# Value projection turned around: weights stationary, 512 positions moving, results turned in 32x32 blocks on the way to memory

## The chip, the core and the metric

The kernel runs on one core of a Trainium2 chip. The metric is the device time of one execution in microseconds (us). The engines of the core are named as the profile names them: PE (matrix products; PEld is its loading of the stationary operand), DVE (vector), ACT (activation), POOL (general), SP (issues transfers). Each has its own queue of instructions and works through it in order; engines wait for each other through semaphores. Transfers (DMA) are issued from the queues of SP, ACT or POOL and carried out by 16 DMA engines.

## What is computed

Two attentions of 32 heads of width 18 over the same 2048 positions of width 576, mixed by a gate:

```python
def _A_ref(x, wqkv, wo):                      # every head has its own q, k, v
    qkv = (x @ wqkv).reshape(B, S, 3, H, Dh)
    p = softmax(einsum("bhqd,bhkd->bhqk", q, k) * Dh ** -0.5)
    return einsum("bhqk,bhkd->bhqd", p, v)  ...  @ wo

def _B_ref(x, wq, wk, wv, wo):                # 32 query heads share one k and one v
    ...

g = sigmoid((x * gate_w).sum(-1, keepdims=True))
return g * a + (1 - g) * b
```

S = 2048, D = 576, H = 32, Dh = 18. All inputs and outputs are float32. The change concerns v of the first attention: 2048 positions by 576 features (32 heads of 18).

## The kernel before, in words

**Units.** The 64 heads are 64 units, u = 0 to 63: the 32 of the shared-key attention (they use the value tile vb), then the 32 with their own keys and values. One step T handles one tile of 128 key positions of one unit, so that there are 1024 steps; the main loop goes two steps at a time. A unit's scores are computed twice: once with queries as stationary operand, only to find each query's maximum (step_max, L525 to L555; the matmul is L540), and, 22 steps later (LEAD), with keys stationary, followed by the exponential on ACT (exps, L586) and the product with the values (step_pv, L614). A block of values of the second attention is the stationary operand of L614: 19 columns, 18 features and a column of ones that sums the probabilities.

**Matrix products in float32.** A product of two float32 tensors is made of three: each operand is split into a high and a low part, and high by high, high by low and low by high are added up. With a contraction over 576 this makes the list PROJ (L37) of 14 matmuls for one result tile. products (L264) runs that list with 128x128 weights stationary and 512 positions of x moving. This is how keys and queries are projected, in 14 weight tiles (MT) by 4 position blocks (project, L339; project_rest, L427).

**The value projection** (project_v, L316) takes it the other way round: 128 positions of x are stationary, and half of the value weights, 288 columns, move. A result tile has positions on the partitions and 288 features along them. There are 32 such units (16 position tiles, 2 halves), each of 14 matmuls (L319). ACT copies a result from PSUM into a tile with 19 columns per head (L322), whose 19th column a memset has filled with ones at the start (L314), and issues on its own queue the transfer to the DRAM tensor v_d (L323), which holds 16 x 128 x (32 x 19) values. The value weights come in as two tiles of 288 columns during the key and query projection (L447 to L454) and are split by ACT and DVE.

**When.** The value units run in the lead, the iterations T = -22 to T = -2, in which only maxima are computed. The text LEADS gives the order of an iteration: "mA0 MA1 mA2 MA3 V.A mB0 MB1 mB2 MB3 V.B". Each m is one maximum matmul (512 keys), followed by a reduction on DVE (L555). V stands for as many value units as keep to the schedule:

```python
while len(vunits) > 32 * (-T - 1 - (c == "B")) // LEAD:
```

So there are 22 half-steps, and each gets one or two units. The maxima of a half-step use PSUM banks 4, 5, 6 and one of the banks 0 to 3; value units take banks 0 to 3 in turn (next_s, next_m). From T = 0 on a written-out order for each pair of steps (FIRST, PLAIN, ONE, TWO, EACH) interleaves scores (s), maxima (m), one maximum over two key blocks at once (c, with its helper x) and value products (p), each with its bank.

**At T = 0** (open_ph2, L494) the pools of the projection are closed and those of the main loop opened in their room; the first two key tiles then get two rows of a constant each (L505). The values of four heads at a time are loaded by load_vg (L509), one transfer of 608 KB, 30 steps before their first use.

**Maxima to score rows.** At the end of a unit's maxima, max_rows (L557) reduces and turns them on DVE, splits them on POOL (L565 to L567), and writes them through a DRAM tensor m_d into two extra rows of the query tile (L569 to L573), all on SP's queue. The scores of that unit, six steps later, need them. Queries of units 3 and up are loaded on SP's queue too (load_q, L124 and L855). A list "slow" advances one piece per iteration, among them the gates (L464).

Of the kernel before, what the change touches and what calls it, by code (L numbers as in the profile page):

```python
# [8 lines left out]
F32 = mybir.dt.float32  # L9
# [40 lines left out]
def gated_mix_kernel(ctx: ExitStack, tc: tile.TileContext, xT, wall, wv, wo, out):  # L50
# [21 lines left out]
    v_d = dram.tile([16, P, H * 19], F32, name="v_d")  # L72
    on_d = [dram.tile([9 * P, S], F32, name=f"on{x}") for x in "hl"]


# [28 lines left out]
    def other():  # L104
        return bk[:, next_s(), :]
# [84 lines left out]
    def load_w(mt, eng=None):  # L190
        st = wpool.tile([P, NKT, P], F32, name="wst", bufs=MT - 2)
        load5(st, wall[mt], eng)
        return st

    def size(n, st):
        for k0, k1, p in ((0, 4, P), (4, 5, 64)):
            nc.vector.tensor_reduce(n[0:p, k0 // 4:k0 // 4 + 1], st[0:p, k0:k1], axis=AX.XY, op=OP.max,
                                    apply_absolute_value=True)
# [110 lines left out]
        nc.vector.tensor_copy(vb[:, 4 * c:4 * c + 4, 0:18],  # L309
                              pv[:, 0:72].rearrange("p (j d) -> p j d", d=18))  # L310

    vst = [vsp.tile([P, 16, 19], F32, name=f"vst{i}") for i in range(3)]
    for t in vst:
        nc.gpsimd.memset(t, 1.0)  # L314

    def project_v(st_, hf, w):  # L316
        fp = other()
        for n, (a, b, k, kr) in enumerate(PROJ):
            nc.tensor.matmul(fp[:, 0:288], X[b][:kr, k, st_ * P:(st_ + 1) * P], w[a][:kr, k, :],  # L319
                             start=(n == 0), stop=(n == len(PROJ) - 1))  # L320
        t = vst[st_ % 3]
        nc.scalar.activation(t[:, :, 0:18], fp[:, 0:288].rearrange("p (h d) -> p h d", d=18), AF.Copy)  # L322
        dma(v_d[st_, :, 304 * hf:304 * hf + 304], t.rearrange("p h d -> p (h d)"), nc.scalar)  # L323

    def run(gen):
        for _ in gen:
# [23 lines left out]
    with tc.tile_pool(name="xs", bufs=6, side="right") as xsp:  # L350
# [61 lines left out]
        for n in range(6, 12):  # L412
# [8 lines left out]
    vwp = ph1.enter_context(tc.tile_pool(name="vwp", bufs=1, side="right"))  # L421
    VS = [None, None]

    for b in (SB, MB):
        dma(ksb[b + 54:b + 56, :], ones_r, nc.gpsimd)

    def project_rest():  # L427
        bal = None
        for n in range(12, len(JOBS)):
            mt, c = JOBS[n]  # L430
            if c == 0 and mt + 1 < MT:
                WP.append(prep_w(W[mt + 1]))
            project(n, gen=bal, at={16: (2, 11)}.get(n, ()))
            for m in range(*AT.get(n, (0, 0))):
                measure_a(m, W[m])
            if n == 13:
                bal = balance(2)
                next(bal)
            if c == 0:
                if mt == 4:  # L440
                    load_k(ksb, ROW_KB, nc.gpsimd)
                    load_kd(kdb, ROW_KB, nc.gpsimd)
                if mt == 5:
                    load_q(0, nc.gpsimd)
                if mt in (6, 7):
                    load_q(mt - 5, nc.gpsimd)
# [47 lines left out]
    def open_ph2():  # L494
        ph1.close()
        L["pt"] = ctx.enter_context(tc.tile_pool(name="ppool", bufs=1, side="left")).tile([P, 16, 512], F32, name="pt")
        L["work"] = ctx.enter_context(tc.tile_pool(name="work", bufs=2, side="left"))
        p2 = ctx.enter_context(tc.tile_pool(name="p2", bufs=1, side="right"))
        L["pool"] = p2
        L["ks"] = [p2.tile([P, S], F16, name=f"ksa{i}") for i in range(2)] + [ksb]  # L500
        L["kds"] = [p2.tile([P, 512], F16, name="kda"), kdb]
        L["oacc"] = p2.tile([P, 16, D], F32, name="oacc")
        for t in L["ks"][:2]:
            for b in (SB, MB):
                dma(t[b + 54:b + 56, :], ones_r)  # L505

    VG = {}
# [49 lines left out]
    def max_rows(u):  # L557


        m = ms[u % 2]  # L560
        nc.vector.tensor_reduce(m[:, 0:16], MX.pop(u), axis=AX.X, op=OP.max, negate=True)
        mt = lead.tile([P, 32], F32, name="mt")
        nc.vector.transpose(mt, m)  # L563
# [3 lines left out]
        nc.gpsimd.tensor_tensor(mh[:, 1, :], mt, mh[:, 0, :], op=OP.subtract)  # L567
        md = m_d[u % 4]
        dma(md, mh.rearrange("p a f -> p (a f)"))  # L569
        for b in (SB, MB) if u > NU - 3 else (SB,):  # L570
            for a in range(2):
                dma(qs[u % 3][b + 54 + a:b + 55 + a, :].rearrange("o (i b f) -> o i b f", b=4, f=32),
                    md.rearrange("(b i) (o a f) -> o a i b f", i=32, o=1, a=2)[:, a, 0:16])  # L573

    PT = {}

# [419 lines left out]
    TAIL = {TL: [N8], TL + 2: [N8], TL + 6: [N8, N8, N8], TL + 8: [HALF[0]], TL + 10: [N8]}  # L996
    for T in range(-LEAD, NSTEP + 2, 2):
        if T == 0:
            open_ph2()
        for f in at.get(T, []) + at.get(T + 1, []):  # L1000
            f()
        M = T + LEAD
        alone = M >= NSTEP
        if M >= 16 and M % 16 == 0 and (T < 0 or alone) and M // 16 - 1 < NU:
            max_rows(M // 16 - 1)
        units = sum(due(t, Tb, Tc, 32) for t in (T, T + 1) for _, _, _, Tb, Tc in SEG)
        if 0 <= T <= TL and not alone:
            steps_pair(T, M, FIRST if T == 0 else pair_order(T))
            units = 0
            order = ""  # L1010
        else:
            order = LEADS if T < 0 else LAST if T > TL else ALONE
        for op in order.split():
            k, second, c = op[0], op[1:2] == "B", op[2:]
            if T == -2 and op == "MB3":
                step_max(*divmod(LEAD, 16), "x")
            if k == "V":
                while len(vunits) > 32 * (-T - 1 - (c == "B")) // LEAD:
                    project_v(*vunits[0], WV[vunits[0][1]])
                    vunits.pop(0)  # L1020
            elif k == "x":
                if M + 2 < NSTEP:
                    step_max(*divmod(M + 2, 16), "x")
            elif k in "mM":
                step_max(*divmod(M + second, 16), int(c), k == "M", T < 0 and c == "3")
            elif k == "s":
                if T >= NSTEP:
                    continue
                if T < TL:
                    step_scores(*divmod(T + second, 16), int(c), alone)  # L1030
                else:
                    h, n = divmod(T + second - TL, 8)
                    step_scores(NU - 1, 2 * n + int(c) // 2, int(c), alone, 2 * h + int(c) % 2)
            elif k == "U":
                pull(min(units, 1))
                units -= min(units, 1)
            elif k == "u":
                if T in LAST_U:
                    next(END_U)
            elif k == "c":  # L1040
                if T == TL + 10:
                    next(HALF[0], None)
            elif T > TL:
                last_pv(T - TL - (2 if k in "pfP" else 1), {"h": (0,), "H": (1,)}.get(k, (0, 1)))
            elif T >= 2:
                step_pv(*divmod(T - (2 if k in "pfP" else 1), 16), 256 * (k in "fH"), 256 if k in "ph" else 512)
                if k in "HQ" and T % 16 == 0 and T < NSTEP:
                    head_out(T // 16 - 1)
        pull(units)
        for f in TAIL.get(T, ()):  # L1050
            next(f, None)
        if slow and M % 16:
            for _ in range(2 if T > 1000 else 1):
                if slow:
                    try:
                        next(slow[0])
                    except StopIteration:
                        slow.pop(0)
# [42 lines left out]
```

## Time and profile before

| | |
|---|---|
| median of 3 runs | 2629.82 us (2628.44 to 2631.03) |
| the profiled execution | 2630.69 us, of which the span in the profile is 2628.9 us |
| PE busy | 2608.2 us, 99% of the span |
| DVE, ACT, POOL busy | 2387.2 (91%), 2368.1 (90%), 282.9 us (11%) |
| first and last value matmul (L319) | begin at 199.8 and 274.9 us |
| value matmuls | 448, 294 ns each by their records |
| ACT's copies of their results (L322) | 32, 410 ns each |
| transfers to v_d | 32 of 152 KB, on ACT's queue |

The span is counted from the first to the last instruction that the profiler saw. A matmul's record covers its way through the array and overlaps that of the next one, so the distance of two starts, not the length of a record, tells what one costs. In groups by line, the columns are: line, engine, operation, output and input tiles, shapes, count | busy time in us, mean ns of one | idle time of the engine just before, and what ended it. The chain of waits is the work that ended last, followed back from the end; its rows are start, length, engine, tile and line. Rows by window give the length, then the busy time of PE, PEld, DVE, ACT and POOL, the granted clock as a share of the full one, and the share and rate of the DMA engines.

### The profile page before, as it was taken

To read this page: it belongs to the slowest core of one execution; us is meant where nothing else is said; L and a number is where in the kernel's file an instruction comes from. 1 tells how busy PE (TensorE), PEld (TensorE's weight loads), DVE (VectorE), ACT (ScalarE), POOL (GpSimd) and SP (SyncE) were. 2 spreads that over 40 slices of the span, in tenths; PEclk is the share of its full clock that TensorE was granted. 3 is DMA by queue.
4 is the path that set the end of the run, shared out by engine and by line. 5 is a ranking of instruction groups with operands and counts; after the bars stand their busy time and mean duration, and the time that the engine had idled before them with its cause. 6 is when DMAs were issued, how large, how long until landed. Compare 5 with 4: busy or idle time off the path is not lost.

```text
span 2628.9 us, 59506 instructions
## 1 busy us (share of the span) xinstructions
PE 2608.2 (99%) x22342; PEld 951.7 (36%) x22342; DVE 2387.2 (91%) x4192; ACT 2368.1 (90%) x4408; POOL 282.9 (11%) x526
## 2 busy tenths in 40 slices
PE   9999999999999999999999999999999999999998
PEld 7788322222222222222223333333333222223444
DVE  7447999999999999999999999999999999998873
ACT  4341899999999999999999999999999999998885
POOL 4640000001000100010111001000100011001000
PEclk9999999999999999999999999999999999999999
DMA  7332000001101100110122113212220122123312
GB/s 203 124 111 83 26 20 18 21 19 50 37 20 32 49 29 20 40 45 20 40 70 78 50 45 93 67 41 56 84 61 23 42 68 74 40 53 103 94 37 96
DMA packets 127310, 150.19 MB, mean 57 GB/s; under 512 B 55456, under 2 KB 94744, under 8 KB 125933
## 3 DMA queue, kind: packets, MB, share of 16 engines
q1 hardware_dynamic: 112593, 119.38, 15.9%
q0 software_dynamic: 8096, 19.30, 2.1%
q10 hardware_dynamic: 6332, 7.71, 0.8%
q8 instruction: 175, 2.87, 0.5%
q14 instruction: 114, 0.93, 0.1%
HBM read 90.80 MB, written 46.45 MB: 52 GB/s over the span
## 4 chain that ended last, share of the span: by engine, by line
PE 93%; DVE 4%; ACT 1%; DMA 1%; issue 1%; SPq 0%; ACTq 0%; DVEq 0%; POOL 0%
PE bk L614 39%; PE bk L599 28%; PE bk L540 15%; PE bk L268 5%; PE bk L764 3%; PE bk L319 2%; DVE junk L546 1%; DVE mx L555 1%; ACT pt L586 1%; DVE norm_a L210 0%; DVE oacc L835 0%; DVE pl L283 0%; PE bk L626 0%; SPq L56 0%; ACT xh L361 0%
## 5 line engine op out<-in xcount | busy, mean ns | idle before, releaser
L586 ACT ACTIVATE pt<-bk 128x512 f32<-128x512 f32 (+1 forms) x3690 | 2076.3, 672 | 48.0 <-PE bk L599 28.2
L555 DVE TENSOR_REDUCE mx<-bk 128x1 f32<-128x512 f32 x2260 | 1424.6, 682 | 68.5 <-PE bk L540 29.4
L599 PE MATMUL bk<-qs,ksb 56*128 56x512 f16 x2688 | 795.6, 380 | 1.0 <-ACT pt L586 0.3
L540 PE MATMUL bk<-ksb,qs 54*128 54x512 f16 x2363 | 721.3, 380 | 1.1 <-ACT pt L586 0.6
L614 PE MATMUL bk<-pt,vb 128*19 128x256 f32 (+1 forms) x6400 | 593.1, 446 | 0.0
L614 PE MATMUL bk<-pt,vg 128*19 128x512 f32 (+1 forms) x5304 | 550.5, 491 | 0.0
L551 DVE TENSOR_REDUCE mx<-bk 128x2 f32<-128x1024 f32 x417 | 507.1, 1216 | 2.0 <-PE bk L540 1.2
L540 PEld LDWEIGHTS <-qs 54*128 54x128 f16 x4096 | 298.8, 93 | 306.6 <-issue 253.5
L599 PEld LDWEIGHTS <-ksb 56*128 56x128 f16 x2688 | 206.3, 93 | 540.9 <-issue 488.6
L599 PE MATMUL bk<-qs,ksa 56*128 56x512 f16 x1408 | 397.0, 380 | 1.3 <-ACT pt L586 0.5
L540 PE MATMUL bk<-ksa,qs 54*128 54x512 f16 x1232 | 381.6, 380 | 0.6
L546 DVE CUSTOM_DVE_ANT_0 junk<-bk,xb 128x512 bf16<-128x512 f32 x501 | 340.9, 680 | 6.9 <-PE bk L599 2.4
L543 ACT ACTIVATE xb<-bk 128x512 f32<-128x512 f32 x501 | 308.8, 616 | 3.9 <-PE bk L540 2.7
L614 PEld LDWEIGHTS bk<-pt,vb 128*19 128x19 f32 x6400 | 111.9, 97 | 267.3 <-issue 251.6
L565 POOL TENSOR_SCALAR mt<-mt 128x32 f32<-128x32 f32 x64 | 18.4, 288 | 1632.7 <-DVE mt L563 1632.7
L599 PEld LDWEIGHTS <-ksa 56*128 56x128 f16 x1408 | 100.8, 94 | 231.3 <-issue 205.1
L614 PEld LDWEIGHTS bk<-pt,vg 128*19 128x19 f32 x5304 | 93.2, 97 | 217.5 <-issue 202.0
L540 PE MATMUL bk<-kdb,qs 54*128 54x512 f16 x373 | 141.0, 378 | 0.2
L277 ACT ACTIVATE ph<-bk,tv 128x512 f16<-128x512 f32 x56 | 38.1, 686 | 96.7 <-PE bk L268 57.5
L283 DVE SCALAR_TENSOR_TENSOR pl<-bk,tv,ph 128x512 f16<-128x512 f32 x56 | 41.7, 749 | 70.1 <-ACT ph L277 42.8
L268 PE MATMUL bk<-xh,wh 128*128 128x512 f32 (+1 forms) x295 | 85.0, 385 | 1.0 <-ACT xh L361 1.0
L268 PE MATMUL bk<-xh,wl 128*128 128x512 f32 (+1 forms) x295 | 84.6, 384 | 0.0
(146 smaller groups left out, 1338.7 us busy)
## 6 DMA issues: line engine op xcount, KB each, us to landing
qs<-qkh SPq DMA_DIRECT2D x244, 72.0 KB
qs<-qkl SPq DMA_DIRECT2D x122, 72.0 KB
onh<-oh SPq DMA_DIRECT2D x32, 256.0 KB
onl<-ol SPq DMA_DIRECT2D x32, 256.0 KB
oih<-onh SPq DMA_DIRECT2D x16, 512.0 KB
oil<-onl SPq DMA_DIRECT2D x16, 512.0 KB
ot<-oe SPq DMA_DIRECT2D x220, 36.0 KB
qkh<-ph POOLq DMA_DIRECT2D x56, 128.0 KB, 2.1
```

The costliest lines, as they stand in the source:

```text
L268: nc.tensor.matmul(bk[:, fp, a0:b0], w[a][:kr, k, :], X[b][:kr, k, s0 + a0:s0 + b0], start=(n == 0), stop=(n == len(PROJ) - 1), skip_group ...
L283: nc.vector.scalar_tensor_tensor(l, fp, t, h, op0=OP.mult, op1=OP.subtract)
L319: nc.tensor.matmul(fp[:, 0:288], X[b][:kr, k, st_ * P:(st_ + 1) * P], w[a][:kr, k, :], start=(n == 0), stop=(n == len(PROJ) - 1))
L540: nc.tensor.matmul(pm, qs[u % 3][b:b + 54, i * P:(i + 1) * P], k, start=True, stop=True)
L543: nc.scalar.activation(MX["x", u, i], pm, AF.Relu)
L546: nc.vector.tensor_tensor_reduce(junk, pm, MX.pop(("x", u, i)), 1.0, -3e38, op0=OP.add, op1=OP.max, accum_out=MX[u][:, i, c:c + 1])
L551: nc.vector.tensor_reduce(flat[:, c0:c0 + len(group)], bk[:, n0:n0 + len(group), :], axis=AX.X, op=OP.max)
L555: nc.vector.tensor_reduce(MX[u][:, i, c:c + 1], pm, axis=AX.X, op=OP.max)
L586: nc.scalar.activation(L["pt"][:, t[0]:t[0] + k, :], bk[:, n:n + k, :], AF.Exp, scale=SCALE / LIFT ** 2)
L599: nc.tensor.matmul(bk[:, n, :], kst(u)[b:b + 56, i * P:(i + 1) * P], qs[u % 3][b:b + 56, x * 512:(x + 1) * 512], start=True, stop=True)
L614: nc.tensor.matmul(acc[32 * j:32 * j + 19, a:b], v_of(u, i), PT[u, i, j][:, a:b], start=(i == 0 and a == 0), stop=(i == 15), skip_group_ch ...
L764: nc.tensor.matmul(fp, *mms[k], start=(k == 0), stop=(k == len(mms) - 1))
```

## The change

- The value weights become stationary: five tiles of 128 features (the last has 64 and is filled up with zeros), loaded into tiles of the kind that the other weights use, when the key and query projection reaches weight tile 9, and split (ACT, POOL, DVE) by prep_w one tile ahead, the first at weight tile 13. A value unit is one weight tile by 512 positions, with products: 20 units of 14 matmuls.
- A result has features on the partitions. ACT copies it to SBUF (128x512), DVE turns each 32x32 block of it (turn_v), and SP's queue gets four transfers a unit (two in the last weight tile), of 32 features each, that write it to v_d. v_d is now 2048 x 576, without a column of ones, and a transfer writes pieces of 32 values. A unit is turned after the second maximum of the next half-step; what is left is turned at T = 0.
- The units are spread over the 22 half-steps by the same formula with 20 in place of 32.
- The value tiles of the main loop get their ones from two memsets at T = 300 (own_rows), where the constant rows of the key tiles are written too. A load of four heads is four transfers of 18 columns each.
- The row maxima of units 0 and 1 and the queries of unit 3 go through POOL's queue instead of SP's.

```diff
+    def load_wv(t):
+        st = wpool.tile([P, NKT, P], F32, name="wst", bufs=MT - 2)
+        m = min(P, H * DH - P * t)
+        src = wv[:, P * t:P * t + m]
+        if m < P:
+            nc.gpsimd.memset(st, 0.0)
+        dma(st[:, 0:4, 0:m], src[0:512, :].rearrange("(k p) m -> p k m", p=P))
+        dma(st[0:64, 4, 0:m], src[512:576, :])
+        return st
...
-    vst = [vsp.tile([P, 16, 19], F32, name=f"vst{i}") for i in range(3)]
-    for t in vst:
-        nc.gpsimd.memset(t, 1.0)
-
-    def project_v(st_, hf, w):
-        fp = other()
-        for n, (a, b, k, kr) in enumerate(PROJ):
-            nc.tensor.matmul(fp[:, 0:288], X[b][:kr, k, st_ * P:(st_ + 1) * P], w[a][:kr, k, :],
-                             start=(n == 0), stop=(n == len(PROJ) - 1))
-        t = vst[st_ % 3]
-        nc.scalar.activation(t[:, :, 0:18], fp[:, 0:288].rearrange("p (h d) -> p h d", d=18), AF.Copy)
-        dma(v_d[st_, :, 304 * hf:304 * hf + 304], t.rearrange("p h d -> p (h d)"), nc.scalar)
+    vst = [vsp.tile([P, 512], F32, name=f"vst{i}") for i in range(2)]
+    vtt = [vsp.tile([P, 512], F32, name=f"vtt{i}") for i in range(4)]
+    VJOBS = [(t, c) for t in range(5) for c in range(4)]
+    turn = []
+
+    def project_v(n):
+
+        t, c = VJOBS[n]
+        if c == 0 and t < 4:
+            WV.append(prep_w(W[MT + t + 1]))
+        w = WV[t]
+        fp = next_s()
+        products(fp, w, 512 * c, 0, 512)
+        st = vst[n % 2]
+        nc.scalar.activation(st, bk[:, fp, :], AF.Copy)
+        touch(fp)
+        turn.append(n)
+
+    def turn_v():
+
+        n = turn.pop(0)
+        t, c = VJOBS[n]
+        o = vtt[n % len(vtt)]
+        nc.vector.transpose(o, vst[n % 2])
+        for a in range(4 if t < 4 else 2):
+            f = P * t + 32 * a
+            dma(v_d[512 * c:512 * c + 512, f:f + 32].rearrange("(b i) j -> i b j", i=32),
+                o[32 * a:32 * a + 32, :].rearrange("i (b j) -> i b j", j=32), VQ[a % len(VQ)])
+
+    VQ = [nc.sync]
...
-                if mt in (7, 10):
-                    hf = (mt - 7) // 3
-                    VS[hf] = vwp.tile([P, NKT, 288], F32, name="vwst")
-                    load5(VS[hf], wv[:, 288 * hf:288 * hf + 288])
-                if mt in (9, 12):
-                    hf = (mt - 9) // 3
-                    WV.append({y: vwp.tile([P, NKT, 288], F32R, name=f"vw{y}{hf}") for y in "hl"})
-                    split_w(VS[hf], WV[hf], nc.vector)
+                if mt == 9:
+                    for t in range(5):
+                        W.append(load_wv(t))
+                if mt == 13:
+                    WV.append(prep_w(W[MT]))
...
+    def own_rows():
         for t in L["ks"][:2]:
             for b in (SB, MB):
                 dma(t[b + 54:b + 56, :], ones_r)
...
+        L["vg"] = [L["pool"].tile([P, 16, 76], F32, name=f"vg{i}") for i in range(2)]
+        for t in L["vg"]:
+            nc.gpsimd.memset(t, 1.0)
 
     def load_vg(g):
-        t = L["pool"].tile([P, 16, 76], F32, name="vg", bufs=2)
-        dma(t, v_d[:, :, 76 * g:76 * g + 76].rearrange("k p c -> p k c"))
+        t = L["vg"][g % 2]
+        for i in range(4):
+            f = DH * (4 * g + i)
+            dma(t[:, :, 19 * i:19 * i + DH], v_d[:, f:f + DH].rearrange("(k p) c -> p k c", p=P))
         VG[g] = t
...
-        dma(md, mh.rearrange("p a f -> p (a f)"))
+        eng = nc.gpsimd if u < 2 else None
+        dma(md, mh.rearrange("p a f -> p (a f)"), eng)
...
-        when(16 * (u - 3) + 17, lambda u=u: load_q(u))
+        when(16 * (u - 3) + 17, lambda u=u: load_q(u, nc.gpsimd if u == 3 else None))
...
+    when(300, own_rows)
...
-    vunits = [(st_, hf) for hf in range(2) for st_ in range(16)]
+    vunits = list(range(len(VJOBS)))
...
         if T == 0:
+            while turn:
+                turn_v()
             open_ph2()
...
-                while len(vunits) > 32 * (-T - 1 - (c == "B")) // LEAD:
-                    project_v(*vunits[0], WV[vunits[0][1]])
-                    vunits.pop(0)
+                while len(vunits) > len(VJOBS) * (-T - 1 - (c == "B")) // LEAD:
+                    project_v(vunits.pop(0))
...
                 step_max(*divmod(M + second, 16), int(c), k == "M", T < 0 and c == "3")
+                if c == "1" and turn:
+                    turn_v()
```

More of the change, by code (lines that the diff above doesn't have):

```diff
@@ L71, in gated_mix_kernel @@
     r_d = dram.tile([NU, S], F32, name="r_d")
-    v_d = dram.tile([16, P, H * 19], F32, name="v_d")
+    v_d = dram.tile([S, H * DH], F32, name="v_d")
     on_d = [dram.tile([9 * P, S], F32, name=f"on{x}") for x in "hl"]
@@ L420, in gated_mix_kernel @@
                 measure_a(mt, W[mt])
-    vwp = ph1.enter_context(tc.tile_pool(name="vwp", bufs=1, side="right"))
-    VS = [None, None]
     for b in (SB, MB):
@@ L502, in open_ph2 @@
         L["oacc"] = p2.tile([P, 16, D], F32, name="oacc")
+    VG = {}
+    def own_rows():
         for t in L["ks"][:2]:
@@ L505, in open_ph2 @@
                 dma(t[b + 54:b + 56, :], ones_r)
-    VG = {}
+        L["vg"] = [L["pool"].tile([P, 16, 76], F32, name=f"vg{i}") for i in range(2)]
+        for t in L["vg"]:
+            nc.gpsimd.memset(t, 1.0)
     def load_vg(g):
-        t = L["pool"].tile([P, 16, 76], F32, name="vg", bufs=2)
-        dma(t, v_d[:, :, 76 * g:76 * g + 76].rearrange("k p c -> p k c"))
+        t = L["vg"][g % 2]
+        for i in range(4):
+            f = DH * (4 * g + i)
+            dma(t[:, :, 19 * i:19 * i + DH], v_d[:, f:f + DH].rearrange("(k p) c -> p k c", p=P))
         VG[g] = t
@@ L572, in max_rows @@
                 dma(qs[u % 3][b + 54 + a:b + 55 + a, :].rearrange("o (i b f) -> o i b f", b=4, f=32),
-                    md.rearrange("(b i) (o a f) -> o a i b f", i=32, o=1, a=2)[:, a, 0:16])
+                    md.rearrange("(b i) (o a f) -> o a i b f", i=32, o=1, a=2)[:, a, 0:16], eng)
     PT = {}
```

## The prediction

> **What bounds the kernel now.** I read the page first: the busy shares and the chain that ended last.
>
> ```profile
> span 2628.9 us, 59506 instructions
> PE 2608.2 (99%) x22342; PEld 951.7 (36%) x22342; DVE 2387.2 (91%) x4192; ACT 2368.1 (90%) x4408; POOL 282.9 (11%) x526
> PE 93%; DVE 4%; ACT 1%; DMA 1%; issue 1%; SPq 0%; ACTq 0%; DVEq 0%; POOL 0%
> PE bk L614 39%; PE bk L599 28%; PE bk L540 15%; PE bk L268 5%; PE bk L764 3%; PE bk L319 2%; DVE junk L546 1%; DVE mx L555 1%; ACT pt L586 1%; DVE norm_a L210 0%; DVE oacc L835 0%; DVE pl L283 0%; PE bk L626 0%; SPq L56 0%; ACT xh L361 0%
> ```
>
> PE is the chain, 93% of it, and the edited line L319 is on it with 2%. So PE time added there, or a PE wait that nothing later absorbs, moves the end. Next I read the chain in order of time around the value stage.
>
> ```profile
> 199.38 0.54 PE bk L540 x4
> ...
> 213.62 0.54 PE bk L540 x4
> 214.16 3.90 PE bk L319 x28
> 218.05 0.54 PE bk L540 x4
> 218.59 2.05 PE bk L319 x14
> 220.64 0.54 PE bk L540 x4
> ...
> 273.11 2.05 PE bk L319 x14
> 276.31 3.54 ACT pt L586 x7
> ```
>
> The value stage runs from 199.4 to 275.1: four row-maximum matmuls (0.54), then one or two value units of 14 matmuls, with hardly a wait between. Two units take 3.90 and one 2.05, so a unit costs 1.85 us and 0.20 goes once per half-step for the switch. The schedule makes 11 iterations (T = -22 to -2) of two half-steps: 22 half-steps, 32 units, 59.2 us of value matmuls.
>
> **The change, part by part.**
>
> *A. The units.* There are now 5 weight tiles by 4 position blocks, 20 units of 14 matmuls, each moving 512 columns. That is 280 matmuls for 448, but 143,360 columns for 129,024, since 576 features fill 4.5 tiles and the half tile streams as long as a whole one. The same form (128x128 stationary, 512 moving, same 14-entry list) already runs at L268. From the timeline there, the first weight load of one unit and of the next:
>
> ```profile
> 120.59 0.89 PEld L268 LDWEIGHTS bk<-xh,wh 128*128 128x128 f32 x4
> 123.85 0.89 PEld L268 LDWEIGHTS bk<-xh,wh 128*128 128x128 f32 x4
> ```
>
> They stand 3.26 us apart. So 20 x 3.26 = 65.2 us replaces 59.2: **+6.0 us**, on the path. The switch disappears in the two half-steps that get no unit: **-0.4**.
>
> *B. DVE in the value stage.* Each unit adds one 128x512 transpose to a DVE that does eight maxima per iteration. The groups by line and form (the first row for the value stage alone):
>
> ```profile
> L555 DVE TENSOR_REDUCE mx<-bk 128x1 f32<-128x512 f32 x88 | 54.4, 681 | 19.1 <-PE bk L540 17.0 <-PE bk L319 1.0
> L563 DVE STREAM_TRANSPOSE mt<-m 128x32 f32<-128x32 f32 x64 | 13.5, 212 | 6.6
> L561 DVE TENSOR_REDUCE m<-mx 128x16 f32<-128x64 f32 x64 | 13.4, 209 | 0.1
> L161 DVE TENSOR_TENSOR wl<-wst,wh 64x128 fp32r<-64x128 f32 x28 | 7.9, 283 | 0.4
> L156 ACT ACTIVATE wh<-wst 128x512 fp32r<-128x512 f32 x14 | 8.7, 624 | 4.4 <-DMA wst<-wall 4.4
> ```
>
> The reductions grow by (681 - 209) / 448 = 1.05 ns per element; from 212 ns at 32 elements a 512-wide transpose is estimated at 212 + 480 x 1.05 = 0.72 us. The far bound is 16 blocks at 212 ns, 3.39. I take 0.72, the slope of the nearest rows. A half-step is then 4 x 0.68 + 0.72 = 3.44 us on DVE against 0.54 + 0.20 + 3.26 = 4.00 on PE: covered. DVE would bind above 4.00 - 2.72 = 1.28 us a transpose. Four half-steps also split a weight tile (2 x 0.283 on DVE: 4.01, even; ACT's copies have idle ACT). Cost 0; above 1.28 us, 20 times the excess.
>
> The Trainium skill, "VectorE: DVE Perf Modes", section "The three transpose paths", gives 311 ns for a 128x128 bf16 transpose. Four of those are an estimated 1.24 us: just under the limit, and two uncovered transposes (C and D below) would add an estimated 1 us to the sum. No run here has yet shown the wide form.
>
> *C. A half-step without a unit.* The loop hands out floor(20k/22), and k = 11 and k = 0 give nothing: T = -12 first half and T = -2 second half. At T = -12 the second four maxima follow the first four at once. They need banks 4 to 6 again. DVE starts 0.3 us after PE, takes two maxima, the transpose placed behind the second, and the third: 0.3 + 3 x 0.68 + 0.72 = 3.1 us until bank 6 is free; PE would have been there after 0.8. **+2.3 us**, and the next unit starts that much later.
>
> *D. The hand-over to T = 0.* The last unit used to stand behind the last maxima, and DVE worked those off under it. From the timeline:
>
> ```profile
> 270.13 5.07 DVE L555 TENSOR_REDUCE mx<-bk 128x1 f32<-128x512 f32 x8 [1.95 <-PE bk L540]
> 275.09 0.39 PE L599 MATMUL bk<-qs,ksb 56*128 56x512 f16 x1
> 276.31 4.03 ACT L586 ACTIVATE pt<-bk 128x512 f32<-128x512 f32 x8 [0.71 <-PE bk L599]
> 276.76 3.08 DVE L555 TENSOR_REDUCE mx<-bk 128x1 f32<-128x512 f32 x5
> 279.90 1.01 PE L540 MATMUL bk<-ksb,qs 54*128 54x512 f16 x2 [0.59 <-ACT pt L586]
> ```
>
> DVE was done at 275.2, when T = 0 began; ACT's exponentials then set the pace and T = 2 began 4.8 us after the last unit. Now the maxima and a transpose come last: DVE ends them 3.9 us after the last unit (four maxima and one transpose, 3.4, begun 0.5 after it), and T = 0 brings it seven more operations, 4.85 us. T = 2 needs a bank of the fifth of them or later: 7.4 to 8.75 us after the last unit. Before, counted with the 0.95 us of the final maxima and the extra L540 that now follow the unit, it was 5.8. So +1.6 to +3.0; **+2.2**, the middle.
>
> *E. Transfers.* The writes of values go from 32 on ACT's queue to 72 on SP's, of 512 pieces of 128 B; each load of values becomes four of 2,048 pieces of 72 B. Nearest rows: the 128-packet store m_d (128 B; a window of 1.5 us) and the old value load (304 B; 5 us).
>
> ```profile
> q1 hardware_dynamic: 144, 0.02, 7.3%
> ...
> q1 hardware_dynamic: 2221, 0.81, 68.9%
> ...
> 1338.22 0.45 SPq L56 DMA_DIRECT2D vg<-v_d  x1
> 1357.43 0.34 SPq L56 DMA_DIRECT2D m_d<-mh  x1
> 1358.89 1.26 SPq L56 DMA_DIRECT2D qs<-m_d  x2
> ```
>
> 0.073 x 16 x 1.5 us / 144 = 12 ns, and 0.689 x 16 x 5 / 2221 = 25 ns a packet. The stores: 36,864 x 12 to 25 / 16 = 28 to 58 us in a stage of 84: covered, by four buffers too. A unit's four issues take 4 x 0.45 to 4 x 0.63, under 2.6 us of each 4.0. A value load takes 8,192 x 12 to 25 / 16 = 6 to 13 us, and the row maxima follow on that queue 19 us later: covered. Cost 0; uncovered, the price is in the rivals.
>
> *F. POOL's queue.* The row maxima of units 0 and 1 and the queries of unit 3 move from SP to POOL.
>
> ```profile
> 1357.16 0.24 POOL L567 TENSOR_TENSOR mh<-mt,mh 128x32 f16<-128x32 f32 x1
> 1364.42 0.09 PEld L599 LDWEIGHTS <-ksb 56*128 56x128 f16 x1 [0.85 <-DMA qs<-qkh]
> ...
> qkh<-ph POOLq DMA_DIRECT2D x56, 128.0 KB, 2.1
> qs<-qkh POOLq DMA_DIRECT2D x12, 72.0 KB, 2.8
> L56 POOL DMA_DIRECT2D qkh<-ph x56 | 30.6, 546 | 47.5 <-ACT ph L277 47.5
> ```
>
> From the maxima on POOL (1357.4 in a typical unit) to the first score (1364.4) are 7.0 us. On POOL: issue 0.55, landing 2.1, two issues 1.1, landing 2.8: 6.5 us. It fits unit 1 with 0.5 to spare, unit 0 has three iterations; POOL blocks meanwhile, with only weight splits and, for unit 3, the maxima of unit 2 nine steps later behind it. Cost 0, at most +1. The standing ones (two memsets and four 8 KB copies at T = 300), the dropped issues on ACT, the memsets saved at the start and the weight loads during the key and query projection lie on engines with idle time there: 0.
>
> Sum: 6.0 - 0.4 + 2.3 + 2.2 = **+10.1 us**. The profiled execution took 2630.7 (span 2628.9 and 1.8 around it), 0.9 over the median of 2629.8. The forecast is 2629.8 + 10.1 = **2639.9**.
>
> **The rivals.** The clock rows by microsecond (columns: window; length, PE, PEld, DVE, ACT, POOL busy; granted clock):
>
> ```profile
> 278.00:279.00 1.00, 0.88 (x5) 0.30 (x5) 1.00 (x3) 1.00 (x3) 0.00 (x0) 1.00 0.03 8
> 279.00:280.00 1.00, 0.41 (x3) 0.12 (x4) 0.83 (x2) 1.00 (x3) 0.00 (x0) 0.60 0.13 33
> 280.00:281.00 1.00, 1.00 (x4) 0.13 (x4) 0.00 (x0) 1.00 (x3) 0.00 (x0) 0.50 0.00 0
> 285.00:286.00 1.00, 1.00 (x9) 0.16 (x8) 0.74 (x2) 0.82 (x1) 0.00 (x0) 0.50 0.00 0
> 286.00:288.00 2.00, 2.00 (x26) 0.50 (x26) 1.51 (x3) 1.68 (x4) 0.00 (x0) 0.99 0.00 0
> ```
>
> After the thin stretch of T = 0 the clock is halved from about 279.2 to 286: 6.8 us, worth 3.4 us of PE.
>
> *1. A second drop at T = -12.* The missing unit leaves PE about 1.1 us of work in 3.4, thinner than the stretch that cost the clock here. For: that row. Against: it is shorter. Price +3.4: 2643. Chance 0.25. The Trainium skill, "TensorE: Matmul & The Clock Gate", section "Why this matters for your kernels", warns only of PE gaps over about 3 us. By that rule C would cost no clock and the sum stays; the trace shows a drop where no PE gap exceeded 0.6 us, so I don't lean on it.
>
> *2. Not slower: the hand-over gets cheaper.* It already loses 3.4 us of clock and over 3 of waiting. If the clock stays at 1.00 through T = 0 to 4 and DVE's backlog falls under the wait for ACT that is there anyway, D is 0 and the drop is gone: 6.0 - 0.4 + 2.3 - 3.4 = +4.5, 2634, inside what can't be told. It decides at whether the clock row reads 1.00 after the last unit. Against: T = 0 gets thinner for PE, not denser. Chance 0.16.
>
> *3. DVE or the stores bind.* Transposes at 3.39 us: 20 x 2.11 = +42 us, 2682. Stores above 84 x 16 / 36,864 = 36 ns a packet fill the buffers; at 50 ns the stage is 115 us, +31, 2671. Both rows speak against. Chance 0.07.
>
> **How the numbers follow.** The forecast has 0.47; 0.05 is left for a gain that I can't name. 0.2%, about what a measurement of this kernel can tell from no change, is 5.3 us. Faster 0.05, same 0.17 (rival 2 and a sliver of the forecast's low end), slower 0.78. The range takes in rivals 1 and 2, the bounds of D, POOL's 1 us and the slower transpose: 2633 to 2648.
>
> **What would show it.** Value units 3.26 us apart with 65 us in all; the transposes near 0.7 us; a PE wait of 2 to 3 us for DVE near the middle of the stage; T = 2 beginning over 7 us after the last unit; the stage near 84 us; the main loop unchanged in length. It is wrong if units come faster than 3.2 us, if the hand-over shrinks, or if PE waits for a transfer in the second half of the units.

## The result, and the profile after

The changed kernel takes 2643.72 us (median of 4, 2642.53 to 2644.95) against 2629.85 of the kernel before: a ratio of 1.0053, 95% interval 1.0041 to 1.0065. It is 13.9 us slower; 2639.9 had been forecast, in a range of 2633 to 2648. The page of the profiled execution (2644.95 us, span 2642.8), busy shares and chain:

```profile
span 2642.8 us, 59309 instructions
PE 2618.8 (99%) x22174; PEld 945.0 (36%) x22174; DVE 2398.0 (91%) x4216; ACT 2368.3 (90%) x4405; POOL 298.5 (11%) x543
PE 88%; issue 3%; POOL 3%; DVE 3%; ACT 1%; DMA 1%; SPq 1%; ACTq 0%; POOLq 0%; DVEq 0%
```

PE has 10.6 us more of busy time. POOL's 3% of the chain is no new cost: the chain now goes back through POOL's queue into the key and query projection, in which PE is busy without a pause beside it (all of 85 to 200 us, in both profiles).

Where the 13.9 us lie can be read from a few events that both profiles have: the first maximum of the value stage (L540, now L569), the last value matmul, and DVE's copy of a finished unit (L636, now L666). Times in us from the start of the span:

| stretch | before | after | difference |
|---|---|---|---|
| start to the first maximum | 199.31 | 201.71 | +2.40 |
| first maximum to the last value matmul (274.86, 284.57) | 75.55 | 82.86 | +7.31 |
| last value matmul to the copy of unit 0 (317.91, 328.50) | 43.05 | 43.93 | +0.88 |
| copy of unit 0 to that of unit 49 | 1759.43 | 1758.66 | -0.77 |
| unit 50 | 35.20 | 38.54 | +3.34 |
| copy of unit 50 to the end | 516.36 | 517.10 | +0.74 |

The -0.77 recurs in e1, e6 and e7 below (-0.70 to -0.78), though not in e3 (-0.02); it nearly cancels the +0.88 above it. No run shows where it and the +0.74 come from.

**The value stage.** The chain in order of time, after:

```profile
230.19 0.54 PE bk L569 x4
230.72 3.46 PE bk L278 x14
234.19 0.54 PE bk L569 x4
...
238.73 3.46 PE bk L278 x14
242.19 0.37 PE bk L569 x2
242.75 0.41 issue
243.16 0.68 DVE mx L584
243.84 0.62 DVE vtt L345
244.46 0.59 DVE mx L584
245.08 0.39 PE bk L569 x2
245.48 3.46 PE bk L278 x14
```

A half-step with a unit is 0.54 + 3.46 = 4.00 us of uninterrupted PE, as forecast (3.26 and the 0.20 of the switch). At T = -12 there is no unit between two groups of maxima: from the first of them at 242.19 to the next unit at 245.48 are 3.29 us, where two groups without a wait take 1.08, so PE waits 2.2 us. The chain names what it waits for: two maxima, the transpose between them, on DVE. The transposes and maxima by line, value stage:

```profile
L584 DVE TENSOR_REDUCE mx<-bk 128x1 f32<-128x512 f32 x90 | 56.9, 675 | 15.9 <-PE bk L569 14.7 <-POOL mx L508 1.0
L345 DVE STREAM_TRANSPOSE vtt<-vst 128x512 f32<-128x512 f32 x20 | 14.0, 702 | 0.0
```

702 ns a transpose; DVE still waits 14.7 us for PE's maxima in this stage, so it has slack.

**The hand-over.** Rows by window (length, then PE, PEld, DVE, ACT, POOL busy, granted clock, DMA share, GB/s):

```profile
286.00:288.00 2.00, 1.00 (x4) 0.28 (x3) 2.00 (x5) 1.41 (x3) 0.00 (x0) 1.00 0.00 0
288.00:290.00 2.00, 1.54 (x7) 0.33 (x7) 2.00 (x5) 0.92 (x2) 0.00 (x0) 0.58 0.44 66
290.00:292.00 2.00, 2.00 (x9) 0.47 (x8) 2.00 (x5) 2.00 (x5) 0.00 (x0) 0.50 0.00 0
294.00:296.00 2.00, 2.00 (x13) 0.21 (x5) 0.87 (x4) 1.10 (x3) 0.00 (x0) 0.71 0.00 0
296.00:298.00 2.00, 2.00 (x25) 0.58 (x26) 2.00 (x4) 2.00 (x4) 0.00 (x0) 1.00 0.00 0
```

DVE is full from 286 to 292 while PE is idle for half of 286 to 288: the backlog of maxima, as forecast. The clock is halved from about 288.3 to 295.1, as long as before (6.8 us), but it now overlaps the wait. The first and the third group of value products, before and after:

```profile
281.84 1.91 PE L614 MATMUL bk<-pt,vb 128*19 128x512 f32 x8
286.60 0.63 PE L614 MATMUL bk<-pt,vb 128*19 128x256 f32 x8
```

```profile
293.63 1.78 PE L644 MATMUL bk<-pt,vb 128*19 128x512 f32 x8
297.18 0.63 PE L644 MATMUL bk<-pt,vb 128*19 128x256 f32 x8
```

Counted from the last value matmul, the first group comes 2.1 us later than before (9.06 us for 6.98) and the third only 0.9: the way between the two takes 3.55 us instead of 4.76, since less of it runs at half the clock.

**Before the stage.** Of the +2.40, about 1.55 are one halving of the clock in the key and query projection, which the profile before does not have (behind PE's wait near 70 us the same hundred matmuls take 24.98 us here and 23.43 there):

```profile
72.00:73.00 1.00, 1.00 (x5) 0.82 (x6) 0.83 (x6) 0.00 (x0) 0.00 (x0) 1.00 0.17 39
73.00:74.00 1.00, 1.00 (x5) 0.75 (x4) 0.75 (x4) 0.00 (x0) 0.00 (x0) 0.64 0.94 272
74.00:75.00 1.00, 1.00 (x4) 0.81 (x3) 0.26 (x1) 0.98 (x2) 0.00 (x0) 0.50 0.00 0
76.00:77.00 1.00, 1.00 (x4) 0.83 (x3) 0.15 (x1) 0.00 (x0) 1.00 (x3) 0.66 0.51 176
```

**Unit 50.** Here stands what nobody had costed. SP's issues around the sixth value load, before and after, then DVE's timeline after:

```profile
2084.54 0.45 SPq L56 DMA_DIRECT2D vg<-v_d  x1
2085.68 0.75 SPq L56 DMA_DIRECT2D sm<-sum_d  x1
```

```profile
2094.36 4.45 SPq L56 DMA_DIRECT2D vg<-v_d  x4
2098.91 1.22 SPq L56 DMA_DIRECT2D sm<-sum_d  x1
```

```profile
2099.20 1.22 DVE L580 TENSOR_REDUCE mx<-bk 128x2 f32<-128x1024 f32 x1
2102.41 0.35 DVE L697 RECIPROCAL sm<-sm 112x32 f32<-112x32 f32 x1 [2.00 <-DMA sm<-sum_d]
2102.68 1.82 DVE L584 TENSOR_REDUCE mx<-bk 128x1 f32<-128x512 f32 x3
```

normalise(6) loads the sums of its rows (sm) at T = 803, right behind the value load at T = 802, and DVE takes their reciprocal two iterations later. The four transfers of 72-byte pieces take SP 4.45 us to issue instead of 0.45 and keep the DMA engines full until 2102. The sums land late, DVE waits 2.0 us with all the maxima behind it, PE runs out of banks, and the clock halves once more:

```profile
2100.00:2102.00 2.00, 1.78 (x20) 0.70 (x17) 0.41 (x1) 2.00 (x5) 0.00 (x0) 1.00 1.25 114
2102.00:2104.00 2.00, 0.64 (x9) 0.14 (x8) 1.59 (x4) 0.74 (x3) 0.00 (x0) 1.00 0.03 8
2104.00:2106.00 2.00, 2.00 (x15) 0.38 (x7) 2.00 (x5) 1.24 (x3) 0.00 (x0) 0.55 0.00 0
```

### The profile page after: what moved, and what is told of

It is laid out like the page before. It is cut to its first block, busy times and chain, and to the rows that moved or that the text cites. A ratio compares the mean times of both kernels' runs of the same rounds, so it can differ in the third digit from the quotient of the medians.

```text
span 2642.8 us, 59309 instructions
## 1 busy us (share of the span) xinstructions
PE 2618.8 (99%) x22174; PEld 945.0 (36%) x22174; DVE 2398.0 (91%) x4216; ACT 2368.3 (90%) x4405; POOL 298.5 (11%) x543
## 4 chain that ended last, share of the span: by engine, by line
PE 88%; issue 3%; POOL 3%; DVE 3%; ACT 1%; DMA 1%; SPq 1%; ACTq 0%; POOLq 0%; DVEq 0%
PE bk L644 39%; PE bk L629 28%; PE bk L569 15%; PE bk L794 3%; PE bk L278 3%; POOL qkh L56 1%; POOL qkl L56 1%; DVE junk L575 1%; DVE mx L584 1%; SPq L56 1%; ACT pt L616 1%; POOL wl L159 0%; POOL qs L56 0%; PE bk L857 0%; PE bk L656 0%
## 5 line engine op out<-in xcount | busy, mean ns | idle before, releaser
L569 PE MATMUL bk<-ksb,qs 54*128 54x512 f16 x2363 | 722.6, 381 | 2.3 <-DVE mx L584 1.8
L569 PEld LDWEIGHTS <-qs 54*128 54x128 f16 x4096 | 299.0, 94 | 313.8 <-issue 259.7
L569 PE MATMUL bk<-ksa,qs 54*128 54x512 f16 x1232 | 382.0, 380 | 0.6
L569 PE MATMUL bk<-kdb,qs 54*128 54x512 f16 x373 | 141.3, 379 | 0.1
L278 PE MATMUL bk<-xh,wh 128*128 128x512 f32 (+1 forms) x395 | 117.3, 394 | 1.7 <-ACT xh L389 1.6
L278 PE MATMUL bk<-xh,wl 128*128 128x512 f32 (+1 forms) x395 | 115.1, 389 | 0.0
```

The source lines that it names most:

```text
L278: nc.tensor.matmul(bk[:, fp, a0:b0], w[a][:kr, k, :], X[b][:kr, k, s0 + a0:s0 + b0], start=(n == 0), stop=(n == len(PROJ) - 1), skip_group ...
L569: nc.tensor.matmul(pm, qs[u % 3][b:b + 54, i * P:(i + 1) * P], k, start=True, stop=True)
```

## The experiments

The theory: value matmuls cost 6 us more, the half-step without a unit 2.2 (the expectations have it at 2.5 and more), the value load 3.3 by delaying the row sums; the rest is small or chance. Ratios are against the kernel before on the same chip. Since a difference of 3 us is about as wide as those intervals, the verdicts rest on the events in the profiles.

**e1: the sixth value load 10 steps earlier.**

```diff
-        when(16 * (H + 4 * g) - 30, lambda g=g: load_vg(g))
+        when(16 * (H + 4 * g) - (40 if g == 5 else 30), lambda g=g: load_vg(g))
```

> The changed kernel with one difference: the load of the values of heads 20 to 23 of the second attention (the sixth value load) starts 10 steps earlier. In the changed kernel's profile that load (four transfers of 72-byte pieces) is followed on the same queue by the row sums that DVE's reciprocal needs, DVE sits idle for 2.0 us, PE runs dry and the granted clock halves; unit 50 takes 38.5 us instead of 35.2. Theory (the small pieces hold up the row sums on the shared queue): units 48 to 50 take the same time as in the kernel before, and the time falls by 3.3 us, to about 2640.4. Rival (a chance drop of the clock, or the load is too slow wherever it stands): a stall of about 3 us stays, here or at the new place, and the time stays at 2643.7.

2640.66 us, ratio 1.0041 (1.0026 to 1.0056); 3.1 us less than the changed kernel. The load is issued at 2055.1, the sums at 2093.6. DVE's copies of units 49 and 50:

```profile
2085.27 0.68 DVE L666 COPY oe<-bk 128x512 f32<-128x512 f32 x1
2120.46 0.68 DVE L666 COPY oe<-bk 128x512 f32<-128x512 f32 x1
```

35.19 us, as before the change, and no wait of DVE for the sums is left. The stall belonged to what stood behind the load, not to the load as such. Whether the sums came late by the 4 us more that SP took to issue the load or by the DMA engines being full, no run tells apart.

**e4: this part of the change alone, in the kernel before.** v_d without the column of ones, four transfers a load, standing ones; value units as they were.

```diff
-        dma(v_d[st_, :, 304 * hf:304 * hf + 304], t.rearrange("p h d -> p (h d)"), nc.scalar)
+        dma(v_d[P * st_:P * st_ + P, 288 * hf:288 * hf + 288], t, nc.scalar)
...
+        for i in range(4):
+            f = DH * (4 * g + i)
+            dma(t[:, :, 19 * i:19 * i + DH], v_d[:, f:f + DH].rearrange("(k p) c -> p k c", p=P))
```

> The kernel before with one part of the change alone: values kept in memory without the column of ones (288 values per row and half), and loaded for four heads by four transfers of 72-byte pieces into tiles whose ones a memset wrote. The value units, their order and the transfers to memory are those of the kernel before. Theory (the small pieces delay the row sums behind the sixth value load): DVE waits 2 us there, unit 50 takes about 38.5 us, and the time rises by 3.3 us, to about 2633.2; nothing else moves. Rival (the stall belongs to the changed value stage or to chance): the same as before.

2633.53 against 2629.70, ratio 1.0014 (1.0004 to 1.0023): +3.8 us. Units 49 and 50, and DVE's wait (in all, times, longest):

```profile
2075.98 0.68 DVE L641 COPY oe<-bk 128x512 f32<-128x512 f32 x1
2115.27 0.68 DVE L641 COPY oe<-bk 128x512 f32<-128x512 f32 x1
```

```profile
DVE sm L672 <- DMA sm<-sum_d: 2.8, 1, 2.8
```

39.3 us for unit 50; the value stage is as long as before (75.33 us). Put in and taken out, the load accounts for 3 to 4 us. Not all of that is the wait itself. In the six profiles with this load in its place DVE waits 2.0 to 2.9 us, and unit 50 takes 2.1 to 5.2 us more than before: 2.1 in e7 below, whose clock stays at 1.00 there, 3.3 to 4.2 in four with one halving of 3.4 us behind the wait, and 5.2 in e3, with two. The copies of e7:

```profile
2089.45 0.68 DVE L666 COPY oe<-bk 128x512 f32<-128x512 f32 x1
2126.71 0.68 DVE L666 COPY oe<-bk 128x512 f32<-128x512 f32 x1
```

**e3: without the transposes.**

```diff
-        nc.vector.transpose(o, vst[n % 2])
+        o = vst[n % 2]
```

> The changed kernel without the 20 transposes on DVE: the untransposed result is written to memory, so the values are wrong and the time is that of everything else. Theory (DVE has slack in every half-step with a unit; 20 transposes of 0.70 us are covered but for the ones at the empty half-step and the hand-over): the empty half-step gets 0.6 to 0.7 us shorter, the hand-over up to 0.7, together 0.7 to 1.4 us. Rival (DVE sets the pace of the stage): up to 14 us less.

Ratio 1.0055 (1.0040 to 1.0070), no less than the changed kernel. In the profile the stage is 82.26 us instead of 82.86, all of it at T = -12 (2.69 us from the first maximum to the unit, where it was 3.29), and the hand-over 43.74 instead of 43.93. So 0.8 us, as the theory said and not 14. In the time it does not show: in this profile the stall at unit 50 is longer (40.4 us) and so is the stretch from unit 0 to unit 49 (by 0.75). DVE's transposes are covered.

**e8: a unit in the empty half-step.**

```diff
-    VJOBS = [(t, c) for t in range(5) for c in range(4)]
+    VJOBS = [(t, c) for t in range(5) for c in range(4)] + [(4, 3)]
```

> The changed kernel with a 21st value unit, a repeat of the last one (it writes the same values again), which by the formula fills the empty half-step of T = -12. Theory (PE waits 2.5 us there for DVE, so a unit fits in): a whole unit of 14 matmuls (3.26 us) costs only about 0.7 us. Rival (the empty half-step costs nothing or is made up later, and the units alone count): 3.3 us more.

Ratio 1.0066 (1.0051 to 1.0081); 3.4 us over the changed kernel by the ratios, so the number of the rival. But the stage is only 1.25 us longer (84.11). That is the mechanism: two successive units are 8.00 us apart across two filled half-steps, and were 6.75 across the empty one. The added unit takes 3.46 us and with it goes a wait of 2.2. (The 0.7 of the expectation left the switch out of the unit and took 2.5 for the wait.) The remainder lies elsewhere: 0.65 at the hand-over and 0.85 more at unit 50, both with clock drops in them, and 0.5 between units 0 and 49; what chance has in it can't be separated with one profile.

**e2 and e11: the matmuls spread evenly.** Value matmuls are handed out singly, 12 or 13 a half-step, so that none is empty and the last one stands at the end.

```diff
-                while len(vunits) > len(VJOBS) * (-T - 1 - (c == "B")) // LEAD:
-                    project_v(vunits.pop(0))
+                while given[0] < 280 * (LEAD + T + 1 + (c == "B")) // LEAD:
+                    next(vunits)
+                    given[0] += 1
```

> The changed kernel with the 280 value matmuls handed out evenly over the 22 half-steps (12 or 13 each) instead of in whole units, so that no half-step is without and the last matmul stands at the end of the stage. Theory (the empty half-step costs 2.5 us, the hand-over costs about what it did before): the stage from its first maximum to the last value matmul, maxima of the last half-step included, is 22 x 0.74 + 65.3 = 81.6 us, no PE wait for DVE inside it, and the hand-over gets about 1 us longer by the last transposes, so the time falls by 1 to 2 us. Rival (what the prediction said: DVE's backlog at the hand-over alone costs 2.2 us): the time falls by 4 to 5 us. Rival (neither place costs anything that is not made up later): the same within 0.5 us.

Ratio 1.0050 (1.0033 to 1.0066): no gain. The stage with the last maxima in it is 83.37 us, over 81.6. The chain shows why (stage of e2):

```profile
231.26 0.68 DVE mx L589
231.94 0.62 DVE vtt L350
232.56 1.18 DVE mx L589 x2
...
234.12 0.62 ACT wh L156
...
234.97 0.07 DVE wl L161
...
236.28 0.29 DVE wl L161
236.59 1.29 DVE mx L589 x2
```

The split of the next weight tile now came right behind the copy of a result; DVE's part waited for ACT's, and the maxima behind it waited too. e11 issues the split in the middle of a unit (and has the earlier value load of e1).

> The changed kernel with the sixth value load 10 steps earlier and its 280 value matmuls spread evenly over the half-steps; unlike the first spread kernel, the split of the next weight tile is issued in the middle of a unit, not right behind the copy of a result, so that DVE does not wait for ACT there. Theory (the empty half-step leaves 2.75 us of a half-step unused by PE, the spread uses it, and only the split was in its way before): the stage from the first maximum to the last value matmul, with the last maxima in it, takes about 81.6 to 82 us instead of 82.9 without them, and the time is 1.5 to 2.2 us under the 2640.7 of the kernel with the earlier load, near 2638.8. Rival (DVE's own load, 75 us of work that begins 2.7 us late, sets the stage): a stage of 83 us or more and the time of the kernel with the earlier load.

2639.53 us, ratio 1.0040 (1.0025 to 1.0055), 1.1 us under e1 by the medians and the same by the ratio. In the profile the stage is 82.24 us with the last maxima in it, and the hand-over 42.76: 125.0 together, against 126.6 in e1. So far the spread gains 1.6 us, with the transposes of the last unit at the hand-over. But the gain does not last: from the copy of unit 0 to that of unit 49 e11 takes 1760.43 us and e1 1758.73, 1.7 more, in steps of some tenths spread over the units, in code that is the same. Where they come from no run shows; e2 has them too (1760.64). So the wait of the empty half-step is real and can be taken out of the stage, but that the whole kernel gets faster by it is not shown.

**e7: row maxima and queries back on SP's queue.**

```diff
-        eng = nc.gpsimd if u < 2 else None
+        eng = None
...
-        when(16 * (u - 3) + 17, lambda u=u: load_q(u, nc.gpsimd if u == 3 else None))
+        when(16 * (u - 3) + 17, lambda u=u: load_q(u))
```

> The changed kernel with the row maxima of units 0 and 1 and the queries of unit 3 back on SP's queue, behind the stores of values. Theory (SP has 2 us of issues per 4 us, so there is no backlog to wait for): the same within 0.5 us. Rival (the stores fill the queue and that is why they were moved): the first scores of unit 1 wait, and the time rises by 1 us or more.

Ratio 1.0050 (1.0035 to 1.0065), 2643.40 us: the same, as far as the interval tells. The trace is finer: from 285 to 420 us neither PE nor its weight loads wait for any transfer, and the copy of unit 0 to that of unit 49 takes 1758.67 us, as in the changed kernel (1758.66). The hand-over is 1.25 us longer in this profile, with the clock halved for 10.2 us instead of 6.8. The move itself costs and brings nothing that can be seen.

**e5, e6, e9, e10: can the clock be held up?** e5 puts ten 128x128 float32 matmuls into T = 0 of the kernel before, e6 into the changed one with e1's load.

```diff
-    FIRST = "s0 m4 s1 c5 s2 m6 s3 m4 s0 m5 s1 m6 s2 m4 s3 x0"
+    FIRST = "s0 m4 s1 c5 D s2 D m6 D s3 D m4 D s0 D m5 D s1 D m6 D s2 D m4 D s3 x0"
...
+            elif k == "D":
+                nc.tensor.matmul(acc[:, 0:P], ident, ident, start=True, stop=True)
```

> The kernel before with ten matmuls of 128x128 more (identity by identity, into a bank that nobody reads before it is written again) between the instructions of T = 0, where PE waits for ACT and DVE and the granted clock then halves for 6.8 us. Theory (the clock falls because PE has too little to do in that stretch, and the halved clock costs 3.4 us): the clock stays at 1.00 and the time falls by 2 to 3.4 us, to about 2627. Rival (the added matmuls only delay the real ones, or the drop has another cause): the drop stays and the time is the same or up to 2 us more.

> The changed kernel with the sixth value load 10 steps earlier, as above, and the same ten matmuls at T = 0. Theory: the clock stays up at the hand-over, 3.3 us from the load and 1 to 3 us from the clock, so 2637 to 2639; still slower than before, since the 6 us of additional value matmuls stay. Rival: as the kernel with the earlier load alone.

e5: ratio 1.0015 (1.0006 to 1.0025), 4.5 us slower by the medians. The clock did stay at 1.00, yet the hand-over is 44.92 us instead of 43.05: a score and a maximum no longer run side by side, and a pair with its added matmuls takes 1.47 us (in e5's timeline, scores at 279.92 and 281.39) where the pairs stood 0.49 apart. These 1.9 us are not the whole of the loss: the profile of e5 also has a halving near 71 us and a longer one near 2593 us. e6: ratio 1.0080 (1.0063 to 1.0096), 10.6 us over e1; here the clock fell first, and the added work ran at half speed (halved for 17.1 us, hand-over 54.2 us).

e9 has four matmuls of the short kind (54 rows, 16-bit, 512 columns) in the gaps, e10 also ten of 256 columns in PE's wait near 70 us.

```diff
+                nc.tensor.matmul(acc, qs[1][MB:MB + 54, 0:P], ksb[MB:MB + 54, 0:512], start=True, stop=True)
```

> The kernel before with four more matmuls at T = 0, of the kind that runs there already (54 rows, 512 columns of 16-bit values, 0.21 us each, into a bank that is written anew before it is read), one in each gap of about 0.28 us that PE has between its pairs. The ten 128x128 ones kept the clock up but stretched T = 0 by more than the clock was worth. Theory (the clock falls for lack of matmuls in one stretch of 3.4 us, and four short ones fit into the gaps): the clock stays at 1.00 through the hand-over and the time falls by 1 to 3 us, to about 2627.5. Rival (four are too few, or each matmul there delays the next): the drop stays and the time is the same or up to 1 us more.

> As the kernel with four short matmuls at T = 0, and ten matmuls of 256 columns more where PE waits 1.5 us for a chain of small DVE instructions near 70 us, behind which the clock fell in 4 of 10 profiles so far. Theory: no drop near 72 us, and the time falls by a further 0.6 us in the mean (4 in 10 of 1.6 us). Rival: the drop near 72 us stays in some executions; the same time as without them.

Ratios 1.0002 (0.9992 to 1.0011) and 0.9999 (0.9990 to 1.0008): no gain. In e9 and e10 the clock at the hand-over is low for about 3.4 us instead of 6.8, and the hand-over takes 42.3 and 42.0 us for 43.05; but it is so in e4 too (42.4), which has no added matmuls, so it can't be credited to them, and the time is the same. The windows of e4:

```profile
280.00:282.00 2.00, 1.83 (x12) 0.27 (x11) 1.65 (x3) 2.00 (x5) 0.00 (x0) 0.72 0.00 0
282.00:284.00 2.00, 2.00 (x13) 0.32 (x12) 0.69 (x1) 0.68 (x2) 0.00 (x0) 0.50 0.00 0
284.00:286.00 2.00, 2.00 (x25) 0.50 (x26) 1.61 (x3) 1.91 (x3) 0.00 (x0) 0.93 0.00 0
```

e10, whose PE gap there is 0.4 us instead of 1.5, shows no drop near 72 us, but neither do seven of the other profiles. No version faster than the kernel before came out of this.

## Why the prediction was right, and where not

**A, the units: right.** 4.00 us a half-step, 3.26 of them value matmuls, from a row of the kernel before. With C it makes up nearly all of the 7.31 us of the stage: 6.0 - 0.4 + 2.2, less the 0.75 of the last five maxima, which now follow the last unit and so fall out of this stretch, is 7.05. Most of the rest lies at the first units: DVE's first reduction begins 2.7 us after the first maximum in both kernels, and one new unit covers that less well than two old ones.

**B, DVE: right.** 702 ns for 720. The Trainium skill's figure ("VectorE: DVE Perf Modes", "The three transpose paths") scaled to 1.24 us was too high here by 0.5; the trace decides.

**C, the empty half-step: right** in mechanism and size (2.2 for 2.3), as far as the stage goes; that it moves the end of the kernel by as much is not shown (e11).

**D, the hand-over: the mis-sized term.** The prediction's "+2.2, the middle", on top of 0.95 for the last maxima, makes 3.15; measured are 0.88. At the prediction's own event, the maximum of T = 2 (279.90 before, 291.68 after), it is 6.8 us after the last unit, under the 7.4 to 8.75 of the forecast and 1.0 over the 5.8 of before. Behind it the sum took the halved clock as a fixed loss beside the wait. It is halved for 6.8 us in both kernels, and after the change more of that time is waiting, in which a slow clock costs nothing: by the third group of value products the delay is down to 0.9, no more than the last maxima that were moved here.

**E, the transfers: the step that failed.** "covered. Cost 0; uncovered, the price is in the rivals." The price of a piece was right (about 6.5 us for the sixth load, 2095.5 to 2102, where 6 to 13 were forecast; 14 ns a packet in the value stage, from 38,544 packets that take 37.5% of 16 engines over 91 us, where 12 to 25 were forecast), but only the row maxima were looked for behind the load. The row sums of normalise(6) stand behind it too, with a DVE instruction that waits for them in order; the trace of before showed them 0.7 us after the old load's issue. e1 and e4 show 3 to 4 us: a wait of 2 to 3 and, behind it, the clock.

**F, POOL's queue: right**, as far as e7 can tell.

**Rival 1, the clock at T = -12,** did not happen in the profiled execution, but in that of e6, which has the same stage:

```profile
242.00:244.00 2.00, 1.38 (x6) 0.96 (x6) 2.00 (x4) 0.00 (x0) 0.00 (x0) 0.92 0.46 67
244.00:246.00 2.00, 2.00 (x7) 1.52 (x6) 1.56 (x3) 0.00 (x0) 0.00 (x0) 0.50 0.84 130
246.00:248.00 2.00, 2.00 (x9) 1.35 (x9) 0.00 (x0) 0.00 (x0) 0.00 (x0) 0.73 0.47 197
```

The stage is 1.55 us longer there (84.40), not 3.4: one stretch of 3.4 us, not two. The waits of PE at T = -12 are the same in both profiles (0.8, 0.2 and 0.6 us); what differs is where they lie, as the last section says. **Rival 2** failed at its own sign, the clock after the last unit; **rival 3** at 702 ns and 14 ns.

So the forecast came 3.8 us low: the stage 0.4 too low, D 2.3 too high, E 3.3 too low, and 2.4 ahead of the stage that were not forecast. That it came so near is in part luck: D and E are off in opposite directions, and about 1.3 of E's 3.3 and 1.55 of the 2.4 are halvings of the clock that not every execution has.

**What stays open** is what lies ahead of the value stage. The clock dropped near 72 us in 5 of 13 profiles (1 of 5 with the old value stage, 4 of 8 with the new one), behind code that the change does not touch. With 1.55 us taken off where it dropped, the first maximum stands at 198.4 to 199.9 us in the one group (199.0 in the mean) and at 199.3 to 201.2 in the other (200.0). So about 1 us may belong to the change; no run takes it apart.

## What to carry to other kernels

Count columns streamed, not instructions: 280 matmuls for 448 were 11% more columns, because a tile filled to half streams as long as a full one (3.46 us for the last unit as for the others), while the weight loads that were saved had been hidden (matmuls of 288 columns stood 0.132 us apart, those of 512 0.233, the same for a column). When a transfer is broken into small pieces, list everything that follows it on its queue within its new length, and for each the in-order engine that waits for it; a wait of 2 to 3 us on a side path became 2 to 5 at the bound, the more the clock fell behind it. A schedule that hands out fewer, larger pieces by rounding leaves slots with none, and the wait in such a slot is set by the engine that the piece had been covering. And follow a gain to the end of the kernel before it is counted: the 1.6 us of e11 were gone by unit 49.

## What the runs showed of the hardware

The granted clock is halved by a thin stretch, not only by a long gap. In all 13 profiles it changes only at points that lie whole multiples of 3.41 us apart (before the change it is full for 273.07 us up to the hand-over, 80 times that, and then half for 6.83), and these points lie elsewhere in each execution. This fits what looked like chance near 72 us, where PE waits 1.5 us, the same in every kernel but e10. In the five profiles with the drop the whole wait lies between two such points. In seven of the eight without it at most 1.4 us of idle time do. The eighth is the kernel before, where the whole wait ends 0.3 us ahead of a point and the clock stays. At T = -12 all 1.6 us of idle time lie between two points in e6, which drops, and at most 1.05 in e1, e7 and the changed kernel, which do not. It is no threshold, though: at the hand-over of the kernel before 0.6 us of idle time between two points were enough, under matmuls of 54 and 56 rows. No run was made to test this reading.

The Trainium skill ("TensorE: Matmul & The Clock Gate", "Why this matters for your kernels") advises against PE gaps over about 3 us; here gaps of 2 us and less were enough.

Filling a thin stretch with full-array matmuls kept the clock up in one kernel (e5) and cost more than it brought, since they broke up the pairs that had run side by side on 54 and 56 rows (0.49 us from pair to pair, 1.47 with the added matmuls).
